# A low table laid out by rows, products joined, squares halved, and a second order by hand

## The chip, the cores and the metric

The kernel runs on one core of one Trainium2 chip. The metric is device time in microseconds (us): the median of several runs of the compiled kernel. Beside the runs there is one profiled execution, whose span (first to last instruction) and engine times the views below come from. The engines are PE (matrix multiply), DVE (elementwise on tensors), ACT (functions and copies), POOL (here only memsets) and SP (here only the issuing of transfers).

## The reference

Two independent layers over a sequence of 2048 rows of 448 columns, side by side in the output. The first is linear attention with learned feature maps; the second a state-space convolution:

```python
    # first: q, k, v from x @ wqkv, 16 heads of 28
    pq, pk = einsum("bhsd,hdf->bhsf", q, w_phi), einsum("bhsd,hdf->bhsf", k, w_phi)
    phi = concat([softmax(p), softmax(-p)])            # of pq and of pk
    kv, z = einsum("bhsf,bhsd->bhfd", phi_k, v), phi_k.sum over s
    a = ((phi_q @ kv) / (phi_q . z + 1e-6)) @ wo
    # second: 448 channels, 256 states each
    dt = exp(log_dt); logdA = dt * (A_re + 1j * A_im)
    P = exp(logdA[:, :, None] * l)                     # l = 0..2047, rounded to bf16
    K = einsum("dn,dnl,dn->dl", Cc, P, dt * Bc).real
    b = irfft(rfft(u) * rfft(K)) + u * Dskip
```

The rounding of l to bf16 leaves 640 distinct positions besides 0, so K is needed at 640 places and not at 2048.

## The kernel before

The kernel splits the position l into a high part (`HI`, 16 values) and a low part (`LO`, 40 values), so that z^l = z^high * z^low for each state's z = exp(logdA). `tables(qt)` does one quarter qt of the channels (QC = 224 columns: 56 pairs of channels by their states) in this order: `rotations` and `dampings` (ACT: sines and exponentials of small multiples), `hi_tables` (DVE: the high table U_ by doubling with z^16, z^32, z^64, z^128), `damp` (DVE: rows 2 to 15 of the low table W as amplitude times rotation), `far` (DVE and ACT: rows 16 to 39), `build_k` (PE: the sum over states, U_ against W, copied out of PSUM) and `scatter_k` (SP: the result to DRAM and back, put by position into KT).

`far` makes rows of W from other rows. A `step(s0, d0, n)` multiplies n complex rows from s0 on by z^256 into rows d0 on: two multiplies (one by the imaginary part into a scratch tile t, one by the real part into W), then a subtraction and an addition. `squares` makes four complex squares: real and imaginary parts squared (two calls of ACT's Square, or DVE), the product of the two parts (DVE) doubled (`scaled`, ACT or DVE), and the difference of the squares (DVE). W is [128, 2, 40, 224]: all rows of the real part, then all of the imaginary part. The powers of z, `PW[k]`, lie as [128, 2, 896].

Around the tables lie the other stages. `signal_spectrum(b)` transforms the signal u against the cosine table G1 on PE and stores it in DRAM. `key_side` makes the attention's sums over keys: per pair of blocks two matmuls, exponentials on ACT, a DMA transpose, matmuls for the softmax sums, a reciprocal and a product on DVE (L612, L613), and matmuls that add up. `query_side(sc)` makes one block of 512 queries: small DVE operations on the scores (L657 to L663), their transpose stored to DRAM by SP and read back four times as SB (L667, L670), and two DVE products by it (L673). `kernel_spectrum(qt)` transforms KT on PE, block b=0 and b=1; its copies go to SK. `conv(qt)` multiplies the two spectra (`prod`, L732, three of 3584 elements), sums real and imaginary parts (`finish`, L738 to L741, or on PE in `finish_pe`), and transforms back (`inverse`).

The order is written out by hand. Every operation is recorded in `Prog` with its engine; at the end `prog.run(ORDER)` issues the recorded operations in the order of a list of numbers, and each engine takes its own in that sequence. `PICKS` holds a letter for each copy, square or scaling that could be on either engine (A is ACT, V is DVE). `PLACES` holds the SBUF address of each tile, and `SLOTS` the PSUM banks. An instruction waits for a count of another engine (or of its own) or for a DMA queue's count; SP's transfers rotate over eight such counts, so that a transfer is issued when the eighth ahead of it has landed. The recording helpers have one line each, so in the views L177 is any two-input DVE operation, L205 any copy, L208 any scaling, L211 any Square, L198 any other activation, L220 any matmul.

Of the kernel before, what the change touches and what calls it, by code (L numbers as in the profile page):

```python
# [10 lines left out]
F32 = mybir.dt.float32  # L11
# [10 lines left out]
N_LO = 40  # L22
# [13 lines left out]
N_KT = 5  # L36
ON_PE = [(0, 1), (1, 1)]
SPLIT = [[(0, QC)]] * 4
# [11 lines left out]
def _dft_tables():  # L50
# [69 lines left out]
def kernel(  # L120
# [227 lines left out]
    q128, q256 = (sb([128, 2, NCOL], F32) for _ in range(2))  # L348
# [16 lines left out]
    for k in LOWP:  # L365
        af(by_states(cs[k][:, 0, :]), from_states(bT), ACT.Sin, scale=float(k), bias=bias_hp)
        af(by_states(cs[k][:, 1, :]), from_states(bT), ACT.Sin, scale=float(-k if k == 8 else k))
        mul(PW[k] if k != 128 else q128, cs[k], amp[k].unsqueeze(1).to_broadcast([128, 2, NCOL]))
        if k == 128:
            copy(PW[128], q128)  # L370
    s2 = sb([128, 2, NCOL], F32)
    square(s2, q128)
    sub(q256[:, 0, :], s2[:, 0, :], s2[:, 1, :])
    stt(q256[:, 1, :], q128[:, 0, :], -2.0, q128[:, 1, :], ALU.mult, ALU.mult)
    copy(view(PW[256][:, 0, 0:1], [56, 32], [1, 2], [2, 28]), view(q256[:, 0, 0:1], [56, 32], [28, 2], [1, 28]))
# [76 lines left out]
    WS = N_LO * QC  # L452
# [41 lines left out]

    def damp(W, A, T, qt, x0, w):
        scaled(A[:, 2:21:3, x0:x0 + w], A[:, 1:20:3, x0:x0 + w], -1.0)
        for part in (1, 0):
            copy(view(W[:, part, 1, x0:x0 + 1], [56, w // 56], [2, 28], [1, 2]),
                 view(PW[8][:, part, qt * QC + x0:qt * QC + x0 + 1], [56, w // 56], [1, 28], [28, 2]))
            mul(view(W[:, part, 2, x0:x0 + 1], [2 * QC, 7], [QC, 2], [1, w]),  # L500
                view(A[:, 0, x0:x0 + 1], [3 * QC, 7], [(1 + part) * QC, 2], [1, w]),
                view(T[:, part, 0, x0:x0 + 1], [QC, 7], [0, 2], [1, w]))

    def far(W, qt, x0, w):
        def pw(i, n):
            return view(PW[256][:, i, qt * QC + x0:qt * QC + x0 + 1], [0, 2], [0, n], [1, w])

        def at(part, row, n):
            return view(W[:, part, row, x0:x0 + 1], [WS, 2], [QC, n], [1, w])

        def rows_(part, row, n):
            return view(W[:, part, row, x0:x0 + 1], [QC, n], [1, w])

        def step(s0, d0, n):
            t = sb([128, 2, n, w])
            mul(t, at(0, s0, n), pw(1, n))
            mul(at(0, d0, n), at(0, s0, n), pw(0, n))
            sub(rows_(0, d0, n), rows_(0, d0, n), t[:, 1])
            add(rows_(1, d0, n), rows_(1, d0, n), t[:, 0])

        def squares(s0, ka, kb, d0):
            def four(part, row, a, b):
                return view(W[:, part, row, x0:x0 + 1], [a * QC, 2], [b * QC, 2], [1, w])
# [6 lines left out]
        copy(view(W[:, 0, 16, x0:x0 + 1], [WS, 2], [1, w]),  # L530
             PW[256][:, :, qt * QC + x0:qt * QC + x0 + w])
# [6 lines left out]
    def hi_tables(qt):  # L538
# [14 lines left out]
        for i, o in ((1, t), (0, U_[:, :, 8:16])):  # L553
            times(o, U_[:, :, 0:8], PW[128][:, i, cols], 16)
# [4 lines left out]
    def build_k(W, U_, TS, c):  # L559
        for j0, nj in ((0, 4), (4, 3)):  # L560
            (b,) = prog.banks(1)
            for j in range(nj):
                items = []
                for i in range(4):
                    nch, ri = i // 2, i % 2
                    for g in range(4):
# [4 lines left out]
                                      view(W[:, ri, 0, x:x + 1], [QC, N_LO], [1, 2]),  # L571
# [215 lines left out]
    def tables(qt):  # L787
# [3 lines left out]
        W = sb([128, 2, N_LO, QC])  # L791
        TS = sb([128, N_LO, 28])
        mset(W[:, 0, 0, :], 1.0)
        mset(W[:, 1, 0, :], 0.0)
        for x0, w in SPLIT[qt]:
            damp(W, A, T, qt, x0, w)
            far(W, qt, x0, w)
            for c in range(x0 // 112, (x0 + w) // 112):
                build_k(W, U_, TS, c)
# [115 lines left out]
```

## Time and profile before

| | |
|---|---|
| median of 3 runs | 238.38 us (238.07 to 239.37) |
| span of the profiled execution | 235.7 us |
| PE busy, matmuls | 208.2 us, 3044 |
| DVE busy, instructions | 218.3 us, 276 |
| ACT busy, instructions | 183.7 us, 312 |
| bytes moved, mean rate | 36.40 MB, 154 GB/s |
| granted TensorE clock | 1.00 all through |

The span and the busy times are of the profiled execution; the runs are 2.7 us longer than its span. Busy time counts a moment once even if two instructions of an engine overlap in it. PE's instructions are pipelined and their ends are modelled, so its busy share does not mean that it is at its limit: in the groups the matmuls of 128x112 take 213 ns, those of 128x448 355 ns.

### The profile page before, as it was taken

How to read it: one execution, taken by the hardware profiler on the slowest of the kernel's cores; microseconds unless marked ns; L12 is line 12 of the kernel's file. 1: busy time of each engine (PE TensorE's matmuls, PEld its weight loads, DVE VectorE, ACT ScalarE, POOL GpSimd, SP SyncE). 2: the span in 40 equal slices, each digit the busy share in tenths (PEclk: the TensorE clock that was granted, in tenths of full speed). 3: DMA queues.
4: the chain of work that ended last, by engine and by line, in shares of the span. 5: the costliest groups of instructions: out<-in, count | busy, mean ns of one | idle time of the engine just before them, and what ended most of it. 6: DMA issues, size and time to landing. Idle time of an engine off the chain costs nothing.

```text
span 235.7 us, 7111 instructions
## 1 busy us (share of the span) xinstructions
PE 208.2 (88%) x3044; PEld 152.1 (65%) x3044; DVE 218.3 (93%) x276; ACT 183.7 (78%) x312; POOL 4.7 (2%) x20
## 2 busy tenths in 40 slices
PE   1338799999898899999998999999999988999993
PEld 2225344656458468677766769765599956787993
DVE  1999999999999899989999999999999899995981
ACT  2999999999999999999999999993337725315420
POOL 2000000000000100000000000000000000000000
PEclk9999999999999999999999999999999999999999
DMA  5899792482978256986449399825784996475952
GB/s 147 213 204 287 132 211 45 157 207 65 298 159 103 59 134 147 178 154 203 139 115 209 25 157 283 217 47 46 234 266 103 165 121 207 32 203 125 209 107 63
DMA packets 81640, 36.40 MB, mean 154 GB/s; under 512 B 65480, under 2 KB 79688, under 8 KB 81224
## 3 DMA queue, kind: packets, MB, share of 16 engines
q1 hardware_dynamic: 81368, 35.71, 69.9%
q8 instruction: 24, 0.39, 0.8%
q10 hardware_dynamic: 240, 0.23, 0.3%
q14 instruction: 8, 0.07, 0.1%
HBM read 19.44 MB, written 8.62 MB: 119 GB/s over the span
## 4 chain that ended last, share of the span: by engine, by line
ACT 28%; DVE 18%; PE 11%; issue 7%; DMA 5%; SPq 0%; DVEq 0%; ACTq 0%
DVE sbuf L177 17%; ACT sbuf L198 13%; PE psum L220 11%; ACT sbuf L205 8%; DMA sbuf<-SCd 4%; ACT sbuf L211 4%; ACT L198 2%; ACT sbuf L208 2%; DMA SCd<-sbuf 1%; SPq L240 0%; DVE sbuf L194 0%; DVE sbuf L189 0%; DVE sbuf L205 0%; DVEq L177 0%; ACTq L198 0%
## 5 line engine op out<-in xcount | busy, mean ns | idle before, releaser
L220 PE MATMUL psum<-sbuf 128*128 128x112 bf16 (+9 forms) x3000 | 206.6, 251 | 23.7 <-ACT sbuf L205 8.8
L177 DVE TENSOR_TENSOR sbuf<-sbuf 128x896 bf16<-128x896 bf16 (+14 forms) x222 | 198.5, 956 | 9.9 <-ACT sbuf L198 5.1
L220 PEld LDWEIGHTS <-sbuf 128*128 128x128 bf16 (+3 forms) x3000 | 149.8, 114 | 79.1 <-issue 16.0
L205 ACT CAST sbuf<-psum 128x448 bf16<-128x448 f32 (+4 forms) x125 | 79.2, 704 | 41.2 <-PE psum L220 40.6
L198 ACT ACTIVATE sbuf<-psum 128x448 bf16<-128x448 f32 (+4 forms) x110 | 63.2, 713 | 1.8 <-PE psum L220 1.7
L211 ACT ACTIVATE sbuf<-sbuf 128x896 bf16<-128x896 bf16 (+1 forms) x16 | 16.5, 1085 | 2.8 <-issue 2.8
L198 ACT ACTIVATE sbuf<-psum,sbuf 128x896 f32<-128x896 f32 (+3 forms) x17 | 13.7, 817 | 0.0
L198 ACT ACT_TABLE_LOAD x8 | 10.3, 1283 | 1.4 <-PEq L899 1.2
L208 ACT ACTIVATE sbuf<-sbuf 128x896 bf16<-128x896 bf16 (+1 forms) x9 | 11.1, 1230 | 0.3 <-DVE sbuf L177 0.3
L205 DVE CAST sbuf<-psum 128x448 bf16<-128x448 f32 (+2 forms) x12 | 7.8, 669 | 2.4 <-PE psum L220 2.4
L215 POOL MEMSET sbuf<- 128x224 bf16 (+4 forms) x15 | 4.3, 314 | 150.4 <-PE psum L220 114.5
L205 ACT COPY sbuf<-psum 112x896 bf16<-112x896 bf16 (+2 forms) x12 | 6.7, 584 | 0.0
L205 ACT COPY sbuf<-sbuf 128x224 bf16<-128x224 bf16 (+2 forms) x13 | 6.1, 476 | 0.0
L177 DVE TENSOR_TENSOR sbuf<-psum,sbuf 128x448 bf16<-128x448 f32 (+3 forms) x12 | 5.0, 442 | 0.0
L194 DVE RECIPROCAL sbuf<-psum 128x64 bf16<-128x64 f32 x8 | 4.4, 549 | 0.2 <-PE psum L220 0.2
L230 PE MATMUL psum<-sbuf 112*112 112x112 bf16 (+1 forms) x44 | 3.5, 216 | 0.0
L230 PEld LDWEIGHTS <-sbuf 112*112 112x112 bf16 (+1 forms) x44 | 2.9, 129 | 0.5
L194 DVE RECIPROCAL sbuf<-sbuf 128x64 f32<-128x64 f32 x4 | 2.2, 545 | 0.0
L189 DVE SCALAR_TENSOR_TENSOR sbuf<-sbuf 128x64 f32<-128x64 f32 (+1 forms) x5 | 1.9, 390 | 0.0
L205 ACT CAST sbuf<-sbuf 128x1792 bf16<-128x1792 f32 x1 | 1.7, 1706 | 0.0
L208 DVE TENSOR_SCALAR sbuf<-sbuf 128x896 bf16<-128x896 bf16 (+2 forms) x4 | 1.6, 401 | 0.0
L205 DVE COPY sbuf<-sbuf 128x448 bf16<-128x448 bf16 (+1 forms) x5 | 1.3, 269 | 0.0
(10 smaller groups left out, 3.0 us busy)
## 6 DMA issues: line engine op xcount, KB each, us to landing
SUd<-sbuf SPq DMA_DIRECT2D x8, 448.0 KB
sbuf<-SCd SPq DMA_DIRECT2D x16, 224.0 KB
sbuf<-SUd SPq DMA_DIRECT2D x4, 896.0 KB
sbuf<-const SPq DMA_DIRECT2D x3, 1024.0 KB
sbuf<-const SPq DMA_DIRECT2D x8, 384.0 KB
sbuf<-in_B_u_dram SPq DMA_DIRECT2D x4, 448.0 KB
out_dram<-sbuf SPq DMA_DIRECT2D x4, 448.0 KB
out_dram<-sbuf SPq DMA_DIRECT2D x16, 112.0 KB
```

Of the source, the lines that this page charges most:

```text
L177: prog.add("V", lambda: nc.vector.tensor_tensor(out=o, in0=a, in1=b, op=op))
L189: prog.add("V", lambda: nc.vector.scalar_tensor_tensor(out=o, in0=a, scalar=s, in1=b, op0=op0, op1=op1))
L194: nc.vector.reciprocal(o, a)
L198: prog.add("A", lambda: nc.scalar.activation(o, a, fn, **kw))
L205: either(lambda: nc.scalar.copy(o, a), lambda: nc.vector.tensor_copy(o, a))
L208: either(lambda: nc.scalar.activation(o, a, ACT.Copy, scale=s), lambda: nc.vector.tensor_scalar_mul(o, a, s))
L211: either(lambda: nc.scalar.activation(o, a, ACT.Square), lambda: nc.vector.tensor_tensor(out=o, in0=a, in1=a, op=ALU.mult))
L215: prog.add("G", lambda: nc.gpsimd.memset(o, v))
L220: nc.tensor.matmul(o, lhsT=l, rhs=r, **kw)
L230: nc.tensor.transpose(o, i, idn)
```

## The change

The change has four parts.

The layout: W becomes [128, 40, 2, 224], the two parts of each row side by side, and the powers PW, q128, q256 and s2 become [128, 4, 2, 224], by quarter. `build_k` reads W with a stride of 448 elements instead of 224.

Joined products: where rows ahead in W can serve as the scratch (n rows behind the destination), a `step` makes both multiplies in one instruction of twice the size: the first step of 7 rows (2 x 3136 become 6272) and the first of 4 rows (2 x 1792 become 3584). The last step of 4 rows has no rows ahead and keeps two. In `hi_tables` the levels 16, 32 and 64 each make one multiply of two. `damp` makes one copy of two; TM is made by two multiplies of 1792 instead of one of 3584.

Halved squares: one activation squares both parts of four rows with a scale of 2^-0.5, which gives half of each square; the doubling of the product goes. Rows so made are smaller by a factor of 2 (and of 8 in the second round), which the constant table F takes back (`GROWN`).

A second order: `ORDER`, `PLACES`, `SLOTS` and `PICKS` are new. The kernel records 969 operations instead of 1008. DVE has 251 instructions instead of 276, ACT 298 instead of 312; PE's 3044 matmuls and the 158 transfers of SP and ACT remain.

```diff
+HALF = 2.0 ** -0.5
+GROWN = {3: 2.0, 4: 8.0}
...
-            F[blk, kt, r] += np.stack([even.real, odd.real, even.imag, odd.imag])
+            F[blk, kt, r] += GROWN.get(kt, 1.0) * np.stack([even.real, odd.real, even.imag, odd.imag])
...
-    PW = {k: sb([128, 2, NCOL]) for k in (8, 16, 32, 64, 128, 256)}
+    PW = {k: sb([128, 4, 2, QC]) for k in (8, 16, 32, 64, 128, 256)}
...
-    mul(TM, CR.unsqueeze(1).to_broadcast([128, 2, 2, NCOL]), PW[8].unsqueeze(2).to_broadcast([128, 2, 2, NCOL]))
+    for i in range(2):
+        mul(TM[:, i].rearrange("p c (q x) -> p c q x", q=4), CR.rearrange("p c (q x) -> p c q x", q=4),
+            PW[8][:, :, i, :].unsqueeze(1).to_broadcast([128, 2, 4, QC]))
...
+    def damp(W, A, T, qt):
+        scaled(A[:, 2:21:3], A[:, 1:20:3], -1.0)
+        copy(view(W[:, 1, 0, 0:1], [56, 8], [2, 28], [1, 2]), view(PW[8][:, qt, 0, 0:1], [56, 8], [1, 28], [28, 2]))
         for part in (1, 0):
...
         def step(s0, d0, n):
-            t = sb([128, 2, n, w])
-            mul(t, at(0, s0, n), pw(1, n))
-            mul(at(0, d0, n), at(0, s0, n), pw(0, n))
-            sub(rows_(0, d0, n), rows_(0, d0, n), t[:, 1])
-            add(rows_(1, d0, n), rows_(1, d0, n), t[:, 0])
+            if d0 + 2 * n <= N_LO:
+                t = W[:, d0 + n:d0 + 2 * n]
+                mul(view(W[:, d0, 0, 0:1], [2 * n * QC, 2], [QC, 2 * n], [1, QC]),
+                    view(W[:, s0, 0, 0:1], [0, 2], [QC, 2 * n], [1, QC]),
+                    view(PW[256][:, qt, 0, 0:1], [QC, 2], [0, 2 * n], [1, QC]))
+            else:
+                t = sb([128, n, 2, QC])
+                for o, i in ((t, 1), (W[:, d0:d0 + n], 0)):
+                    mul(o.rearrange("p n i x -> p (n i) x"), W[:, s0:s0 + n].rearrange("p n i x -> p (n i) x"),
+                        PW[256][:, qt, i, :].unsqueeze(1).to_broadcast([128, 2 * n, QC]))
+            sub(W[:, d0:d0 + n, 0, :], W[:, d0:d0 + n, 0, :], t[:, :, 1, :])
+            add(W[:, d0:d0 + n, 1, :], W[:, d0:d0 + n, 1, :], t[:, :, 0, :])
 
         def squares(s0, ka, kb, d0):
-            sq = [sb([128, 4, w]) for i in range(2)]
-            for i in range(2):
-                square(sq[i].rearrange("p (a b) x -> p a b x", a=2), four(i, s0, ka, kb))
-            mul(four(1, d0, 2, 1), four(0, s0, ka, kb), four(1, s0, ka, kb))
-            scaled(rows_(1, d0, 4), rows_(1, d0, 4), 2.0)
-            sub(rows_(0, d0, 4), sq[0], sq[1])
+            sq = sb([128, 4, 2, QC])
+            af(sq.rearrange("p (a b) i x -> p a b (i x)", a=2), four(s0, 0, 2, ka, kb), ACT.Square, scale=HALF)
+            mul(four(d0, 1, 1, 2, 1), four(s0, 0, 1, ka, kb), four(s0, 1, 1, ka, kb))
+            sub(W[:, d0:d0 + 4, 0, :], sq[:, :, 0, :], sq[:, :, 1, :])
...
             t = sb([128, 2, 8, n, 2, 28])
-            for i in range(2):
-                times(t[:, i], U_[:, :, s0:s0 + n], PW[k][:, i, cols], 2 * n)
+            mul(t.rearrange("p r s n i x -> p r s (n i) x"),
+                view(U_[:, 0, s0, 0, 0:1], [0, 2], [N_HI * 56, 8], [28, 2 * n], [1, 28]),
+                view(PW[k][:, qt, 0, 0:1], [QC, 2], [28, 8], [0, 2 * n], [1, 28]))
...
-                                      view(W[:, ri, 0, x:x + 1], [QC, N_LO], [1, 2]),
+                                      view(W[:, 0, ri, x:x + 1], [2 * QC, N_LO], [1, 2]),
...
-        W = sb([128, 2, N_LO, QC])
+        W = sb([128, N_LO, 2, QC])
...
-    "3 0 41 1 2 42 44 60 35 62 61 5 30 33 58 49 8 9 43 50 59 7 52 55 51 53 57 6 54 80 81 71 63 47 56 48 45 70 82 78 "
+    "35 1 2 67 0 3 5 41 42 44 45 43 49 6 50 60 9 58 52 53 51 7 54 56 62 8 57 61 70 55 65 71 39 77 78 40 46 4 37 63 "
...
```

More of the change, by code (lines that the diff above doesn't have):

```diff
@@ L36 @@
 N_KT = 5
+HALF = 2.0 ** -0.5
+GROWN = {3: 2.0, 4: 8.0}
 ON_PE = [(0, 1), (1, 1)]
-SPLIT = [[(0, QC)]] * 4
 def _round_bf16(a):
@@ L344 @@
     LOWP = (128, 16, 8, 32, 64)
-    PW = {k: sb([128, 2, NCOL]) for k in (8, 16, 32, 64, 128, 256)}
+    PW = {k: sb([128, 4, 2, QC]) for k in (8, 16, 32, 64, 128, 256)}
     amp = {k: sb([128, NCOL], F32) for k in LOWP}
     cs = {k: sb([128, 2, NCOL], F32) for k in LOWP}
-    q128, q256 = (sb([128, 2, NCOL], F32) for _ in range(2))
+    q128, q256 = (sb([128, 4, 2, QC], F32) for _ in range(2))
     CR = sb([128, 2, NCOL])
@@ L451 @@
     ANGLES = [(4, 1, 3, 1), (2, 2, 0, 2), (1, 4, 1, 1)]
-    WS = N_LO * QC
     def args(src, qt):
@@ L493, in dampings @@
         return A
-    def damp(W, A, T, qt, x0, w):
-        scaled(A[:, 2:21:3, x0:x0 + w], A[:, 1:20:3, x0:x0 + w], -1.0)
+    def damp(W, A, T, qt):
+        scaled(A[:, 2:21:3], A[:, 1:20:3], -1.0)
+        copy(view(W[:, 1, 0, 0:1], [56, 8], [2, 28], [1, 2]), view(PW[8][:, qt, 0, 0:1], [56, 8], [1, 28], [28, 2]))
         for part in (1, 0):
[L498 to L502, printed above, removed]
@@ new lines, in damp, with far, four @@
+            mul(view(W[:, 2, part, 0:1], [4 * QC, 7], [2 * QC, 2], [1, QC]),
+                view(A[:, 0, 0:1], [3 * QC, 7], [(1 + part) * QC, 2], [1, QC]),
+                view(T[:, part, 0, 0:1], [QC, 7], [0, 2], [1, QC]))
+    def far(W, qt):
+        def step(s0, d0, n):
+            if d0 + 2 * n <= N_LO:
[10 more added lines that the diff above has]
+            add(W[:, d0:d0 + n, 1, :], W[:, d0:d0 + n, 1, :], t[:, :, 0, :])
+        def squares(s0, ka, kb, d0):
+            def four(row, part, n, a, b):
+                return view(W[:, row, part, 0:1], [2 * a * QC, 2], [2 * b * QC, 2], [1, n * QC])
+            sq = sb([128, 4, 2, QC])
+            af(sq.rearrange("p (a b) i x -> p a b (i x)", a=2), four(s0, 0, 2, ka, kb), ACT.Square, scale=HALF)
+            mul(four(d0, 1, 1, 2, 1), four(s0, 0, 1, ka, kb), four(s0, 1, 1, ka, kb))
+            sub(W[:, d0:d0 + 4, 0, :], sq[:, :, 0, :], sq[:, :, 1, :])
+        copy(W[:, 16], PW[256][:, qt])
@@ L553, in hi_tables @@
         for i, o in ((1, t), (0, U_[:, :, 8:16])):
-            times(o, U_[:, :, 0:8], PW[128][:, i, cols], 16)
+            times(o, U_[:, :, 0:8], PW[128][:, qt, i, :], 16)
         sub(U_[:, :, 8:16, 0, :], U_[:, :, 8:16, 0, :], t[:, :, :, 1, :])
@@ L790, in tables @@
         A = dampings(qt)
-        W = sb([128, 2, N_LO, QC])
+        W = sb([128, N_LO, 2, QC])
         TS = sb([128, N_LO, 28])
         mset(W[:, 0, 0, :], 1.0)
[L794 to L799, printed above, removed]
+        mset(W[:, 0, 1, :], 0.0)
+        damp(W, A, T, qt)
+        far(W, qt)
+        for c in range(2):
+            build_k(W, U_, TS, c)
         scatter_k(qt, TS, KT[qt])
```

26 lines of the change are left out of this document (8 added, 18 removed), and 100 rows, old and new, of tables (ORDER, PLACES, SLOTS).

## The prediction

> **What bounds the kernel now.** I read the page's busy times and slices first, then the table of waits, then the chain of waits at its end, then the groups by line with shapes kept apart.
>
> ```profile
> PE 208.2 (88%) x3044; PEld 152.1 (65%) x3044; DVE 218.3 (93%) x276; ACT 183.7 (78%) x312; POOL 4.7 (2%) x20
> ...
> DVE  1999999999999899989999999999999899995981
> ACT  2999999999999999999999999993337725315420
> ```
>
> DVE is full in every slice between the first and the last few. ACT is as full for two thirds of the span and half empty after. So the question is what DVE does and what it waits for. In the table of waits (engine and line waiting, what released it, total us, times, longest) DVE's rows are:
>
> ```profile
> DVE sbuf L177 <- ACT sbuf L198: 5.1, 3, 4.1
> ...
> DVE sbuf L177 <- ACT sbuf L205: 2.6, 2, 2.4
> DVE sbuf L205 <- PE psum L220: 2.4, 2, 1.3
> ...
> DVE sbuf L177 <- ACT sbuf L211: 0.6, 1, 0.6
> DVE sbuf L177 <- DMA sbuf<-SCd: 0.6, 1, 0.6
> ...
> DVE sbuf L194 <- PE psum L220: 0.2, 1, 0.2
> ```
>
> They sum to 11.5 us. 4.1 (the first dt) and 1.3 (the first matmuls) are start-up; 1.0 of the third row comes after the last finish; 2.4 is one wait at 212 to 215 us. That leaves 2.7 us of small waits in the middle. The chain of waits (start, length, what) shows the 2.4 and what follows it:
>
> ```profile
> 199.47 14.29 PE psum L220 x207
> 213.78 0.98 ACT sbuf L205 x2
> 214.78 2.03 DVE sbuf L177
> 216.91 4.18 DVE sbuf L177 x5
> 221.65 2.56 DVE sbuf L177 x2
> 224.24 2.04 DVE sbuf L177
> 226.30 1.17 DVE sbuf L177 x2
> 227.49 0.64 DVE sbuf L177
> ```
>
> PE runs the last quarter's kernel spectrum behind other work, ACT copies it, and only then DVE's first product (214.78) starts. Now read the joints. 221.65 is an 896 and a 3584 that don't need each other: 0.614 + 2.019 = 2.63 by the rows below, yet the pair takes 2.56, so neighbours overlap by 0.077 (the groups agree: 44 instructions of 1081 ns make 47.6 us, but 46.4 busy). 224.24 is the add that needs the product directly ahead: it starts 0.03 after that one's end, with no overlap. 216.91 starts 0.10 after its product. So a DVE instruction that needs the one right ahead costs 0.11 us (0.077 + 0.034) or, where another wait sits on it too, 0.18 (0.077 + 0.10). This is the row that decides my forecast.
>
> ```profile
> L177 DVE TENSOR_TENSOR sbuf<-sbuf 128x1792 bf16<-128x1792 bf16 x44 | 46.4, 1081 | 0.5 <-ACT sbuf L205 0.3
> L177 DVE TENSOR_TENSOR sbuf<-sbuf 128x3584 bf16<-128x3584 bf16 x23 | 46.1, 2019 | 2.4 <-ACT sbuf L205 2.4
> L177 DVE TENSOR_TENSOR sbuf<-sbuf 128x896 bf16<-128x896 bf16 x74 | 43.5, 614 | 1.1 <-ACT sbuf L211 0.6
> ...
> L211 ACT ACTIVATE sbuf<-sbuf 128x896 bf16<-128x896 bf16 x15 | 14.7, 1038 | 2.8 <-issue 2.8
> ...
> L208 ACT ACTIVATE sbuf<-sbuf 128x896 bf16<-128x896 bf16 x6 | 6.3, 1044 | 0.3 <-DVE sbuf L177 0.3
> ```
>
> From 614 to 1081 ns, 896 more elements cost 467: 0.521 ns an element and 147 ns fixed, or 70 once the overlap is taken off. So two multiplies joined save 0.07 us.
>
> **The change, part by part.** The sum is made on the profiled execution: span 235.7 against a median run of 238.38, so 2.7 us lie around it, and I add differences to 238.38.
>
> *Joined multiplies.* Per quarter `far`'s 3136 pair and its first 1792 pair become one each, as do three pairs of `hi_tables`: 5 instructions fewer, 20 in all, 20 x 0.07 = -1.4 us of DVE. No row has 6272 elements or this form (one input broadcast over two dimensions). Lower bound: by the line above, 3.41 us; upper: the f32 row of 1792 (2.02 us), twice the pace, +3.2 us each. The nearest rows are products of 3584 that already broadcast both inputs and lie on the line (2019 against 2014), so I take the line.
>
> *Squares by the scale.* Six ACT scalings of 896 (1044) and two on DVE (about 0.4 by the L208 DVE row) go; pairs of Squares (1038 each) become one of 1792, which the f32 Square's row, 1794, prices. ACT loses about 6 x 0.87 + 8 x 0.2 = 6.8 us. A Copy with a scale (1044) costs what a Square without does (1038), so the scale is free.
>
> *Engine choices.* Onto DVE: the f32 Square of z^128 (f32 row of that size, 2.02), the cast of PW[128] (1.17 by the other such cast), one damping scale (0.6), two spectrum copies (0.6 each), one build copy. Off it: one bf16 Square (0.61), the two scalings, two AT copies (0.55 each), six small copies (0.2 each). Net of these about +2.0. TM's product in two: +0.07. All DVE work together +0.6 us (-1.4 + 2.0), give or take 0.7.
>
> *The new order on DVE.* The listing of the built kernels says which instructions wait on DVE's own count for the instruction directly ahead. Before it is 14 of 276, and none of them ahead of 174 us: the order put something between every product and its sums. After it is 77 of 251: a product and its subtraction, the subtraction and the square, R and VR, all in a row. Two of the 77 lie in the start-up. 15 carry a further wait. (75 - 15) x 0.115 + 15 x 0.18 = 9.6 against 11 x 0.115 + 3 x 0.18 = 1.8 before: +7.8. Where the further wait is long satisfied the price may be the lower (+6.8), and for query-side instructions of 64 elements the overlap lost may be less than 0.077 (lower end +6.2). I take +7.3.
>
> [...]
>
> *Waits that go.* DVE, slower by 0.1 us each step, falls behind what it waited for. The mid waits' 2.7 us go, and with some 12 waits 12 x 0.077 of lost overlap: -3.6. The 2.4 us at 212: from the last table's end DVE has 19.6 us of work to its first product, now plus six joints, 20.3; PE's queue from the first `build_k` matmul to the last first-block spectrum is 18.2 us by its pitches (19.0 before, and the query multiply it waited for at 200 us is done 30 us earlier), then a copy of 0.6: no wait. -2.4.
>
> *Waits that come.* CR's second copy moves ahead of other work on DVE and stands directly behind PE's last raw product: +0.5, with every start-up product queued behind it. On SP, seven of x's transposes, PID and all of u pass ahead of G1 (1 MB); in the first 24 us the DMA engines moved 215 GB/s, and 5.4 MB up to G1's end make 25 us, or 30 if the transposes go slower. DVE gives the spectrum its first input at about 27 (21 us of work and 6 of waits; before 22), so PE starts its heavy phase some 4 us later. Its cover: PE has 197 us of streaming in 236, DVE gets the key side's sums about 16.6 us of queue after PE, and PE may run 23 to 24 us late in its queue before that costs DVE anything; 27 - 8 = 19, plus the 3 to 5 it lost up to there before. The first query block's four SB reads now stand behind the next block's score store on SP (issue about 122, needed about 130; landing took 6 to 10 us): 0 to 2. Together I take +0.9. POOL's memsets are far ahead of their users. `build_k` reads W at twice the stride; no row shows that, its 896 matmuls (256 ns) may cost nothing or, if a tenth more, 0.4 in the last quarter.
>
> Sum: +0.6 + 7.3 - 3.6 - 2.4 + 0.9 = +2.8, so 241.2 us (span 238.5).
>
> **The rivals.**
> (1) *A wait on the instruction ahead costs nothing in the middle of the kernel*, where the trace has none. Then DVE stays in front of ACT and PE and keeps about 1 us of the old waits: 0.6 - 3.6 - 2.4 + 1 + 0.9 = -3.5, 234.9, faster. For it: ACT's 7 us and the shorter tail queue are real. Against: ten joints of plain kind in the trace and not one without its 0.11. It decides below 0.045 us a joint. 8%. [...]
> (2) *Half is absorbed*: joints 0.06 on average, +3.8 in place of 7.3: 237.7; or the work sums to 0.7 less and the joints take their lower end: 239.4. About no change. 14%.
> (3) *The late start bites*: G1 or u lands after 32 rather than 27. Each us beyond some 30 then shifts PE's key side and DVE one for one: at 33, +3, 244. For it: 1 MB moved behind seven transposes on queues that are 90% busy. Against: it starts as soon as the eighth transfer ahead has landed, while before it waited for a DVE read till 17. 14%.
> (4) *The joined multiply isn't cheaper*: 6272 and the five-dimensional 3584 off the line by a fifth, some 24 us of such work: +5, 246. Nothing in the rows speaks for it. 3%.
>
> **How the numbers follow.** The forecast has 61%. A measurement of this kernel can't tell less than 0.5% (1.2 us: 237.2 to 239.6) from no change. Faster: 8% and a little of (2), 10%. Same: the rest of (2) and the forecast's lower edge, 13%. Slower 77%. Range: below 238.0 lies 12%, above 244.0 some 8%; the forecast's own is 239.6 to 243.0.
>
> **What would show it.** In the profile after: DVE's 251 instructions busy for some 223 us although their work grows by 0.6 only (busy time counts an overlap once, so each joint adds its 0.077); no wait of DVE over 1 us between the start-up and the last finish; runs of DVE in the timeline broken by gaps of 0.03 to 0.1 at products and their sums; the 2.4 us before the last quarter's first product gone; ACT near 175. Wrong would be: DVE's neighbours overlapping although one waits for the other (1), a wait of DVE L194 or L177 on PE of over 1 us at 75 to 100 us (3), a joined 3136 pair over 3.6 us (4).

## The result and the profile after

The changed kernel takes 246.74 us (median of 4 runs, 244.60 to 248.04) against 238.43 us before: a ratio of 1.0345, with a 95% interval of 1.0288 to 1.0403. It is slower, as forecast, but by 8.3 us where 2.8 were forecast, and the time lies above the range. Ratios, here and below, compare fast runs alone, while a median is of all runs, so a ratio is not always the quotient of the two medians beside it. The profiled execution has a span of 245.4 us (235.7 before); it belongs to the run of 247.50 us. In the runs of this study one run takes 1.6 to 2.1 us more than its own span, not the 2.7 that the prediction took from a span and a median of different runs. Its page, busy times and slices:

```profile
PE 214.0 (87%) x3044; PEld 154.8 (63%) x3044; DVE 224.0 (91%) x251; ACT 178.6 (73%) x298; POOL 4.7 (2%) x20
...
PE   1354899999999999999798989998699999999973
...
DVE  1899999999999999999997999999797999999981
ACT  2989999999999998999987769767405545233320
...
PEclk9999999999999999999999999999799999999999
```

DVE is busy for 5.7 us longer with 25 instructions fewer. New are the 7s in its row at slices 22, 29 and 31, and one 7 in the granted clock of TensorE, in slice 29, behind a 6 in PE's own row. The helpers stand one line further down in this kernel: L178 is any two-input DVE operation, L206 any copy, L221 any matmul. The table of waits (engine and line waiting, what released it, total us, times, longest) names the waits behind these slices:

```profile
PE psum L221 <- issue: 4.3, 3, 3.3
...
DVE sbuf L178 <- PE psum L221: 1.7, 1, 1.7
DVE sbuf L178 <- ACT sbuf L206: 1.6, 1, 1.6
DVE sbuf L178 <- DMA sbuf<-SCd: 1.6, 1, 1.6
...
DVE sbuf L178 <- DVE sbuf L206: 0.2, 1, 0.2
```

The wait of the last quarter's product, 2.4 us of the row "DVE sbuf L177 <- ACT sbuf L205: 2.6" of before, is gone; what is left of it is the 0.2 of the last line (the 1.6 behind ACT here is another product's). In its place stand three single waits of 1.6 to 1.7 us: at 134.07 for the score reads of query block 0, at 174.49 (the damping of quarter 3) for PE, at 187.50 (the product of quarter 1) for a copy that follows PE. The last two have one origin, which the chain of waits shows (start, length, what):

```profile
166.28 4.46 PE psum L221 x193
170.74 3.35 issue
174.09 12.33 PE psum L221 x80
186.93 0.55 ACT sbuf L206
187.50 2.57 DVE sbuf L178 x2
```

PE stops for 3.35 us in the middle of one `build_k` operation (8 of its 16 matmuls are done), with no semaphore that it waits for. In the busy times by stretch (us, PE, PEld, DVE, ACT, POOL with instructions, granted clock, DMA share, GB/s), cut at the stop:

```profile
150.00:170.70 20.70, 20.58 (x359) 14.34 (x357) 20.46 (x23) 16.12 (x24) 0.00 (x0) 1.00 0.76 172
170.70:174.10 3.40, 0.05 (x6) 0.01 (x4) 2.13 (x2) 0.62 (x1) 0.00 (x0) 1.00 1.22 188
174.10:177.70 3.60, 3.60 (x26) 2.20 (x27) 3.21 (x2) 2.57 (x6) 0.50 (x2) 0.53 1.05 437
```

In the second row PE is busy for 0.05 us and the DMA engines' share is 1.22; in the third the clock that PE is granted is 0.53 over 3.6 us (by the clock records 0.50 for 3.41 us from 174.28 on). In the kernel before PE never stops for more than 1.2 us after 82 us (the longest is the 1.16 us at 198.31), and its clock is 1.00 all through.

The joints (DVE instructions that need the one directly ahead) are seen in DVE's timeline (start, length; one row is a run of one form without a gap):

```profile
100.55 0.55 DVE L195 RECIPROCAL sbuf<-psum 128x64 bf16<-128x64 f32 x1
101.13 3.06 DVE L178 TENSOR_TENSOR sbuf<-sbuf 128x1792 bf16<-128x1792 bf16 x4
104.11 0.55 DVE L195 RECIPROCAL sbuf<-psum 128x64 bf16<-128x64 f32 x1
104.69 4.41 DVE L178 TENSOR_TENSOR sbuf<-sbuf 128x1792 bf16<-128x1792 bf16 x5
```

The reciprocal of 104.11 starts 0.08 us before the run ahead of it ends (101.13 + 3.06 = 104.19): these neighbours, of which neither needs the other, overlap. Each product that needs its reciprocal (101.13, 104.69) starts 0.03 us after that has ended.

Whole rows of DVE add up to the span, and that is the best way to see where the time went. Busy time is the page's; gaps under 0.15 us before an instruction are short gaps, longer ones waits; the tail runs from DVE's end to the span's end (all us, added up from the traces of this and the experiments):

| | joints | busy | short gaps | waits up to 25 us | waits later | tail | span |
|---|---|---|---|---|---|---|---|
| before | 14 | 218.3 | 1.1 | 6.1 | 5.4 | 4.9 | 235.7 |
| after | 77 | 224.0 | 3.3 | 6.1 | 6.8 | 5.3 | 245.4 |
| e1 | 77 | 223.9 | 3.6 | 6.2 | 7.5 | 4.5 | 245.6 |
| e2 | 33 | 219.8 | 1.6 | 11.1 | 8.7 | 5.0 | 246.2 |
| e3 | 77 | 224.2 | 3.3 | 5.9 | 9.8 | 5.1 | 248.3 |
| e4 | 77 | 224.3 | 3.4 | 5.9 | 6.7 | 4.9 | 245.2 |
| e5 | 16 | 216.5 | 0.8 | 6.2 | 8.0 | 4.6 | 236.1 |
| e6 | 57 | 222.1 | 2.6 | 6.1 | 5.4 | 5.1 | 241.3 |
| e7 | 38 | 220.2 | 1.8 | 6.1 | 3.9 | 4.7 | 236.7 |
| e8 | 77 | 223.9 | 3.3 | 6.0 | 3.5 | 5.1 | 241.8 |
| e9 | 57 | 222.0 | 2.6 | 6.1 | 2.3 | 5.1 | 238.1 |
| e10 | 39 | 220.6 | 2.0 | 6.1 | 8.2 | 5.1 | 242.1 |
| e13 | 14 | 218.8 | 0.9 | 6.2 | 6.7 | 4.5 | 237.1 |
| e14 | 16 | 216.7 | 0.8 | 6.2 | 9.0 | 4.6 | 237.2 |

After against before: busy and short gaps +7.9, waits +1.5, tail +0.4, together (but for rounding) the 9.7 us between the two spans. Each row is one execution. Those of e5 and e9 were the fastest of their runs (237.80 against a median of 238.88, 240.10 against 241.76), that of e10 the slowest (243.90 against 242.51), so spans of different rows differ by more, or less, than the medians do.

### The profile page after: what moved, and what is told of

It reads as the page before. It is cut to its first block, busy times and chain, and to the rows that moved or that the text cites. A ratio compares the mean times of both kernels' runs of the same rounds, so it can differ in the third digit from the quotient of the medians.

```text
span 245.4 us, 7066 instructions
## 1 busy us (share of the span) xinstructions
PE 214.0 (87%) x3044; PEld 154.8 (63%) x3044; DVE 224.0 (91%) x251; ACT 178.6 (73%) x298; POOL 4.7 (2%) x20
## 4 chain that ended last, share of the span: by engine, by line
DVE 43%; PE 21%; ACT 16%; DMA 10%; issue 7%; SPq 1%; DVEq 0%; ACTq 0%
DVE sbuf L178 41%; PE psum L221 20%; ACT sbuf L199 9%; ACT sbuf L206 6%; DMA sbuf<-const 4%; DMA sbuf<-SCd 3%; DMA sbuf<-sbuf 2%; DMA sbuf<-in_B_A_re_dram 2%; DVE sbuf L195 1%; SPq L241 1%; ACT L199 1%; DVE sbuf L206 0%; DVE sbuf L209 0%; DVEq L178 0%; DVE sbuf L190 0%
## 5 line engine op out<-in xcount | busy, mean ns | idle before, releaser
L221 PE MATMUL psum<-sbuf 128*128 128x112 bf16 (+8 forms) x3000 | 212.0, 254 | 24.8 <-DVE sbuf L178 11.3
L178 DVE TENSOR_TENSOR sbuf<-sbuf 128x896 bf16<-128x896 bf16 (+12 forms) x203 | 200.7, 1037 | 11.7 <-ACT sbuf L199 3.4
L221 PEld LDWEIGHTS <-sbuf 128*128 128x128 bf16 (+3 forms) x3000 | 152.5, 115 | 82.1 <-issue 18.4
L206 ACT CAST sbuf<-psum 128x448 bf16<-128x448 f32 (+4 forms) x125 | 77.4, 679 | 53.1 <-PE psum L221 51.8
L199 ACT ACTIVATE sbuf<-sbuf 128x1792 bf16<-128x1792 bf16 (+1 forms) x9 | 13.8, 1537 | 2.2 <-DMA sbuf<-in_B_log_dt_dram 1.5
L206 DVE CAST sbuf<-psum 128x448 bf16<-128x448 f32 (+2 forms) x12 | 7.9, 674 | 3.4 <-PE psum L221 3.4
L206 ACT COPY sbuf<-sbuf 128x448 bf16<-128x448 bf16 (+1 forms) x14 | 7.8, 572 | 3.2 <-PE psum L221 3.2
L206 ACT COPY sbuf<-psum 112x896 bf16<-112x896 bf16 (+2 forms) x13 | 6.9, 533 | 2.6 <-DVE sbuf L178 2.1
L178 DVE TENSOR_TENSOR sbuf<-psum,sbuf 128x448 bf16<-128x448 f32 (+3 forms) x12 | 4.9, 439 | 0.0
L209 ACT ACTIVATE sbuf<-sbuf 128x1568 bf16<-128x1568 bf16 x2 | 3.1, 1544 | 0.0
L206 DVE CAST sbuf<-sbuf 128x1792 bf16<-128x1792 f32 x2 | 2.3, 1126 | 0.0
L213 DVE TENSOR_TENSOR sbuf<-sbuf 128x1792 f32<-128x1792 f32 x1 | 2.0, 2017 | 0.0
L209 DVE TENSOR_SCALAR sbuf<-sbuf 128x1568 bf16<-128x1568 bf16 (+1 forms) x3 | 1.5, 504 | 0.0
## 6 DMA issues: line engine op xcount, KB each, us to landing
sbuf<-SCd SPq DMA_DIRECT2D x16, 224.0 KB
```

Source lines behind the costliest of these rows:

```text
L178: prog.add("V", lambda: nc.vector.tensor_tensor(out=o, in0=a, in1=b, op=op))
L199: prog.add("A", lambda: nc.scalar.activation(o, a, fn, **kw))
L206: either(lambda: nc.scalar.copy(o, a), lambda: nc.vector.tensor_copy(o, a))
L209: either(lambda: nc.scalar.activation(o, a, ACT.Copy, scale=s), lambda: nc.vector.tensor_scalar_mul(o, a, s))
L213: lambda: nc.vector.tensor_tensor(out=o, in0=a, in1=a, op=ALU.mult))
L221: nc.tensor.matmul(o, lhsT=l, rhs=r, **kw)
```

## The experiments

Every kernel was run against the kernel before on the same chip, and each ratio below is to that. The order edits are shown as pieces of an engine's sequence in ORDER, by operation number; unless said otherwise nothing but ORDER differs. In the recorded expectations VectorE is DVE, TensorE is PE and ScalarE is ACT; both names are used from here on.

**e1: the joints alone, in the kernel before.** VectorE's sequence of before, permuted by up to 4 places until it has the changed kernel's 77 joints. One piece of it:

```diff
-630 631 799 633 632 507 508 635 509 634 567 637 566 510
+630 631 633 632 799 507 508 509 566 635 634 637 510 511
```

> The kernel before with nothing but DVE's own sequence changed: neighbours swapped by up to four places, so that 77 of its 276 instructions wait for the one directly ahead (14 before), no load or PE or ACT sequence touched. 63 more joints x 0.117 = 7.4 us. Theory A (a joint costs 0.117 us, and DVE, now later, no longer meets its old waits of 2.7 in the middle and 2.4 at 212 us): 238.4 + 7.4 - 5 = 240.5 to 242. Theory B (the joints cost that, but DVE carries PE and ACT along with it, so the old waits stay): 244.5 to 246. Theory C (a joint is free): 238 to 239.

Measured: 246.84 us, ratio 1.0338 (1.0290 to 1.0386). The time is above what all three theories allowed. The old mathematics with 77 joints is as slow as the changed kernel, but not by its joints alone. By the table busy and short gaps grow by 8.1 us for 63 joints, 0.13 each. The old waits shrink (the last product's from 2.37 to 1.00), but the permutation made one of its own: the queries' small operations came later, and VectorE waited 4.37 us for the score reads of block 0, until 136.72. (PE also waited 3.55 us for a load at 127.23 and had half its clock for 6.83 us from 129.32 on.) The price of a joint is shown; the total isn't a clean sum.

**e2: the joints taken out of the changed kernel.** The same by up to 5 places the other way, 77 down to 33:

```diff
-489 488 490 491 433 435 615 492 493 436 614 772 710 709
+489 488 433 490 491 615 492 435 493 436 614 772 709 710
```

> The changed kernel with DVE's sequence alone altered by swaps of up to five places: 33 joints instead of 77, every other engine's sequence and all transfers as they were. 44 x 0.117 = 5.1 us. Theory A (joints are the largest part of the loss): 246.7 - 5.1 = 241.6, DVE busy down by 44 x 0.077 = 3.4 to some 220.6. Rival (DVE only waits elsewhere, since PE's late second half and the score reads set the time): 244.5 to 246.5 with DVE's idle up by what its joints gave back.

Measured: 247.51 us, ratio 1.0364 (1.0308 to 1.0419). Busy and short gaps fall by 5.8 us for 44 joints, again 0.13 each, and all of it is lost: 5.0 us to waits at the start, where the permutation put instructions ahead of loads and results that they need, and the rest to PE, which stops for 3.27 us at 171.57 and has half its clock for 6.83 us behind it. The time is above both theories. As a test of the total it failed by its own start.

**e3: the score reads of block 0 ahead of the next block's store on SP.**

```diff
-717 497 500 499 465
+497 500 499 717 465
```

> The changed kernel with three of the first query block's four SB reads moved on SP ahead of the next block's score store, behind which they stood. Theory: DVE's wait of 1.6 us on these reads at 132 us goes or shrinks to under 0.4, time -1 to -1.6 (245.1 to 245.7). Rival (it is taken back by the PE stall at 171 us or by the ACT copies behind it): no change, 246.5.

Measured: 248.62 us, ratio 1.0395 (1.0313 to 1.0476). The wait of 1.57 us at 134 goes and comes back as one of 1.65 us at 142, for the reads of the next block. PE's stop stays (3.48 us at 172.09), and the waits of VectorE behind it are longer here (3.02 and 2.73 us). The interval overlaps the changed kernel's, so no change in time is shown: here one block's reads were had sooner at the next block's cost.

**e4: the loads around PE's stop spread.** The stop comes just behind ten transfers that SP issues between 162.4 and 170.2 us: four score reads, three transposed loads of u, a signal spectrum of 896 KB (733) and the two halves of GI (529, 528) of 1 MB each. Four of them moved:

```diff
-882 883 880 881 737 574 733 734 529 528 669 668 940 896 670
+733 574 882 883 880 881 737 734 669 668 940 896 528 529 670
```

> The changed kernel with the burst of loads at 162 to 170 us thinned out on SP: SU of the second quarter and one u transpose go ahead of the third block's SB reads, the two GI loads (1 MB each) go behind the third quarter's scatter. Theory P (PE's stall of 3.35 us in the middle of one build_k operation, at 170.7, is instruction fetch held up by that burst): the stall shrinks to under 1.5, DVE's waits of 1.7 each at 172.8 and 185.9 shrink, time -2 to -3.5 (243 to 245). Rival (the stall comes with the pace of build_k, wherever the loads are): stall still over 2.5, time unchanged or up to 1 us longer, should GI come late for the first inverse.

Measured: 246.74 us, ratio 1.0346 (1.0292 to 1.0400): no change in time. But PE's stop shrank from 3.35 to 0.94 us, no half clock followed it, and the wait of 1.66 us went. GI now came late: PE stood 2.65 us at 182.78 before the first inverse transform, the clock fell to half for 3.41 us behind that, and VectorE waited 1.68, 1.07 and 0.90 us later on. So the stop did what theory P said and the time (243 to 245 us expected) did not: the gain was given back by the cure.

**e5: the mathematics without the order.** The changed kernel's functions with the order, places, banks and engine choices of before, mapped operation by operation. The one edit besides these lists gives the squares' scratch a place in rows of W that are not written yet:

```diff
-            sq = sb([128, 4, 2, QC])
+            sq = W[:, d0 + 4:d0 + 8]
```

> All of the change's mathematics and layouts (rows side by side, joined products, squares halved by the activation's scale, the far copy and the damp copy joined), but in the order of before: each operation stands where before had it, two that were joined where the first of them stood, a halved square where the later of the two squares stood; places, banks and engine choices are those of before, and the squares' scratch lies in rows of the table that are not written yet. 254 VectorE instructions against 276 before and 251 after, and 16 that wait for the one directly ahead (14 before, 77 after). Theory order (the 8.3 us come from the new order alone, its joints and the waits that it makes): the joined products save 1.4 us of VectorE, the scalings and squares that leave it about another 1, so 235.5 to 237.0 us. Theory maths (a product, copy or square costs more in the new form than its row says): 240 us or more. Theory cover (VectorE's saved work only lengthens its waits for TensorE): 238.0 to 238.8 us.

Measured: 238.88 us against 237.93 before, ratio 1.0085 (1.0043 to 1.0127). So all but 1 to 2 of the 8.3 us (0.95 by the medians, 2.0 by the ratio) come with the new order and the places, banks and engine choices that belong to it; these four are not told apart here. The mathematics does save VectorE its 1.8 us (busy 216.5 against 218.3), but the waits grow by 2.7 us. Its rows in the table of waits:

```profile
DVE sbuf L178 <- ACT sbuf L199: 6.6, 7, 4.2
DVE sbuf L178 <- ACT sbuf L206: 3.4, 2, 3.1
```

The first has 4.2 of start-up and 2.4 of exponentials and joined squares that ACT hands over no earlier than before; the second is the last quarter's product, 3.1 where before had 2.4. Of the three theories cover came nearest (238.0 to 238.8 us).

**e6: fewer joints, cleanly.** As e2, but with the first 45 VectorE instructions and those of the queries held in place; 77 down to 57:

```diff
-367 368 770 427 429 428 370 371 373 374 431 612 613 432
+367 368 427 770 429 428 370 371 373 374 612 431 432 613
```

> The changed kernel with VectorE's own sequence permuted by at most 5 places so that 57 instead of 77 instructions wait for the one directly ahead; the first 45 VectorE instructions and those of the queries keep their order, other engines' sequences and the queues are untouched. Theory J (joints are paid on the path that sets the end): 20 x 0.115 = 2.3 us less, 244.4 us. Theory P (TensorE's stop at 171 us and its half clock set the end): VectorE waits instead, 246.0 to 247.4 us.

Measured: 243.69 us against 237.93, ratio 1.0272 (1.0231 to 1.0313). Busy and short gaps fall by 2.5 us, 0.125 a joint, and nothing takes it back. The time falls somewhat further than theory J's 244.4, because the block-0 score wait (1.57 us) is gone as well. PE's stop (3.50 us at 167.43, half clock for 3.41 us) is still there. So these 20 joints were paid on the path that sets the end.

**e7: more joints in the kernel before, cleanly.** 14 up to 38:

```diff
-627 451 626 452 628 453 379 629 380 383 382 455 798 454
+627 626 628 629 451 452 453 379 380 383 382 455 798 454
```

> The kernel before with VectorE's own sequence permuted by at most 6 places so that 35 to 38 instead of 14 instructions wait for the one directly ahead; the first 45 and those of the queries keep their order. Theory J: 22 to 24 x 0.115 = 2.6 us more, less what its middle waits (2.7 us) take up: 239.5 to 241.2 us. Theory hidden (the middle waits take all of it): 238.0 to 239.0 us. Above 242: the permutation made a wait of its own, as in the first such run.

The run had 38. Measured: 238.92 us against 237.93, ratio 1.0048 (1.0024 to 1.0072). 24 joints add 2.6 us of busy and short gaps (0.11 each) and take 1.5 us out of the waits; the span grows by 1.0. The time itself lies in the range of the theory "hidden", but the kernel before was faster in this round than the 238.4 us that the ranges start from; the 1.0 us over it lie between the two theories (up to 0.6, and from 1.1 on). So the waits of this row paid about half of these 24 joints.

**e8: the loads spread without making GI late.**

```diff
-882 883 880 881 737 574 733 734 529 528 669 668 940 896 670 672
+733 574 882 883 880 881 737 734 528 669 668 940 896 670 672 529
```

> The changed kernel with four loads moved on SP: the first quarter's spectrum load and one transposed load stand ahead of the last query block's score reads (some 8 us earlier), the first half of the inverse tables stays, and their second half goes four transfers later. Theory P (TensorE's stop of 3.35 us in the middle of one operation at 171 us is an instruction fetch behind a burst of loads, and the half clock behind it follows from the stop): the stop is under 1.2 us, no half clock follows, the wait of 1.62 us at 187.5 is gone: 243.0 to 245.0 us. If the second half of the tables now comes late, TensorE waits at the first inverse transform instead and the time stays within 246 to 247.5 us. Theory J alone: no change, 246.7 us.

By the edit three loads change place (733, 574 and 529), and the second half of the tables goes six transfers later. Measured: 243.16 us against 237.93, ratio 1.0247 (1.0209 to 1.0284), as theory P had it. PE's timeline at the place of the stop:

```profile
164.83 5.97 PE L221 MATMUL psum<-sbuf 112*128 112x448 bf16 x231
171.65 4.65 PE L221 MATMUL psum<-sbuf 128*32 128x80 bf16 x39 [0.85 <-issue]
```

The stop is 0.85 us, no half clock follows, and both waits of VectorE (1.66 and 1.62) are gone: its waits after 25 us fall from 6.85 to 3.45 us. The stop was worth 2.3 us by the two ratios, 3.1 by the medians (8.3 and 5.2 us over before).

**e9: both edits.** The sequence of e6 with the transfers of e8.

> The changed kernel with both edits that helped: 57 instead of 77 instructions of VectorE that wait for the one directly ahead (the sixth run's sequence), and the loads spread on SP (the eighth run's). Theory two causes (the joints and TensorE's stop with its half clock are separate terms of the 8.3 us): the gains of the two runs, some 3.0 and 3.5 us, add up: 239.7 to 241.0 us against 246.7 of the changed kernel. Theory one cause (either edit only shifts the same wait): no better than the better of the two, 243.0 us or more.

Measured: 241.76 us against 237.63, ratio 1.0158 (1.0126 to 1.0190). By the ratios e6 gains 0.73 points, e8 0.98, both together 1.87, each give or take 0.7. The interval of e9 lies below those of e6 and of e8, so either edit gains on top of the other: joints and stop are two separate causes. That the gains add up in full is not shown so closely: by the medians, each less its own before, they are 2.6, 3.1 and 4.2 us, and 241.76 lies between the two ranges that were expected. VectorE has hardly a wait left in this kernel; its two largest rows:

```profile
DVE sbuf L206 <- PE psum L221: 3.4, 4, 1.3
DVE sbuf L178 <- ACT sbuf L199: 3.4, 1, 3.4
```

Both are start-up and tail but for 0.6 at 202 us. The span of its profiled execution is 2.4 us over before (the medians differ by 4.1): busy and short gaps are 5.2 over, waits 3.1 under.

**e10: 39 joints with the transfers of e8.** A piece against e8:

```diff
-714 774 775 776 617 777 616 618 619 501 502 871 872 873
+714 774 616 775 617 776 777 619 501 618 502 871 872 873
```

> As the ninth run, but with 39 instead of 57 instructions that wait for the one directly ahead; the first 30 VectorE instructions and those of the queries keep their order but for shifts of up to 2 places. Theory J: another 18 x 0.115 = 2.1 us less than the ninth run, 237.6 to 239.2 us. Theory cover (TensorE's own row of work sets the end once VectorE has less to do, as in the fifth run): no less than 239.5 us.

Measured: 242.51 us against 237.63, ratio 1.0211 (1.0184 to 1.0238), no gain. Busy and short gaps fall by another 2.0 us, but VectorE now comes early to score reads (1.21 us at 130, 2.56 at 138) and to a copy behind PE (1.61 at 206). (Its profiled execution also had half the clock from 17.7 to 31.3 us, behind the start-up's stops.) The time is in the range of the theory cover, but its account fits only in part: what came back is waits for transfers and for PE, not PE's row alone.

**e11 and e12: the last quarter's spectrum ahead of an inverse transform on PE.** In the kernel before and in e5, one PE operation moved:

```diff
-772 775 927 947 975 967 963 971 757
+772 775 927 975 967 963 971 947 757
```

> The kernel before with one TensorE operation moved: the inverse transform of 36 matmuls (1.94 us) that stands ahead of the last quarter's first four spectrum operations goes behind them. The last quarter's product, which waits 2.37 us for the copy of their result, then waits some 0.4 us. Theory V (VectorE's row sets the end there): 1.0 to 1.9 us less, 236.0 to 237.0 us. Theory E (TensorE is without gaps there, so its own row sets the end): within 0.5 us of the kernel before.

> The fifth run's kernel (the change's mathematics in the order of before) with the same move on TensorE. Its last quarter's product waited 3.07 us; after the move some 1.1. Theory V: 1.5 to 1.9 us less than the fifth run, and so under the eleventh run by what of the 1.8 us of saved VectorE work is not taken by waits for ScalarE. Theory E: as the fifth run, 238.4 to 239.2 us.

Measured: 238.75 and 239.08 us against 237.63, ratios 1.0044 (1.0023 to 1.0064) and 1.0030 (1.0001 to 1.0058). The first lies above both its theories, the second in theory E's range. The product's wait did not shrink (2.98 and 3.19 us): on ACT, the copy of the moved transform still stood ahead of two of the spectrum's copies and held them up. Here the move on PE's queue alone brought the product nothing (before waits 2.37 us, e5 3.07).

**e13 and e14: the same, with the two copies moved on ACT.**

```diff
-926 754 976 968 948 972 964 928
+926 754 976 968 972 964 948 928
```

> The eleventh run's kernel with two more moves, on ScalarE: the last two of the first four copies of the last quarter's spectrum stand ahead of the copy of the inverse transform that was moved on TensorE, which held them up. The last quarter's product then waits some 0.5 us (2.37 in the kernel before, 2.98 in the eleventh run). Theory V (VectorE's row sets the end): 236.0 to 237.2 us. Theory E (TensorE's row without gaps sets the end, so the wait comes back behind it): 237.3 to 238.8 us, as before.

> The same moves in the kernel with the change's mathematics in the order of before. The product's wait falls from 3.1 to some 1.2 us. Theory V: 236.2 to 237.4 us, and with the 1.8 us of saved work at or under the thirteenth run. Theory E: 237.8 to 239.2 us, as the fifth run.

Measured: 238.33 and 238.72 us against 237.84, ratios 1.0019 (0.9989 to 1.0049) and 1.0023 (0.9995 to 1.0051). The product's wait fell to 0.98 and 1.38 us, and the time did not follow; both lie in theory E's ranges. VectorE's timeline at the end of e13 and then of e14, and PE's in the same order:

```profile
215.14 2.02 DVE L177 TENSOR_TENSOR sbuf<-sbuf 128x3584 bf16<-128x3584 bf16 x1 [0.98 <-ACT sbuf L205]
...
223.64 6.47 DVE L177 TENSOR_TENSOR sbuf<-sbuf 128x3584 bf16<-128x3584 bf16 x6 [0.80 <-ACT sbuf L205]
...
231.99 0.62 DVE L205 CAST sbuf<-psum 128x448 bf16<-128x448 f32 x1 [1.21 <-PE psum L220]
```

```profile
215.14 2.03 DVE L178 TENSOR_TENSOR sbuf<-sbuf 128x3584 bf16<-128x3584 bf16 x1 [1.38 <-ACT sbuf L206]
...
223.64 6.47 DVE L178 TENSOR_TENSOR sbuf<-sbuf 128x3584 bf16<-128x3584 bf16 x6 [0.80 <-ACT sbuf L206]
...
231.99 0.62 DVE L206 CAST sbuf<-psum 128x448 bf16<-128x448 f32 x1 [1.21 <-PE psum L221]
```

```profile
201.60 32.06 PE L220 MATMUL psum<-sbuf 112*128 112x448 bf16 x523 [0.94 <-issue]
...
201.60 32.06 PE L221 MATMUL psum<-sbuf 112*128 112x448 bf16 x523 [1.15 <-issue]
```

The first kernel's VectorE is busy for 2.1 us more than the second's, and both run the end at the same hundredths: PE starts 523 matmuls at 201.60 and runs them without a gap, and there its row, by way of ACT's copies, sets the time. Theory E's "without gaps" holds only from that point on: up to it PE stood 0.94 and 1.15 us with no semaphore to wait for (more on such stops at the end). So the saved VectorE work of the mathematics ends in waits, and the wait taken away before the product comes back as 0.31, 0.80 and 0.17 more behind it (e13). No kernel of this study was faster than the kernel before.

## Why the prediction was right and wrong

*VectorE's work, +0.6: right.* The row that decided the fourth rival stands on the line (3.41 forecast):

```profile
L178 DVE TENSOR_TENSOR sbuf<-sbuf 128x6272 bf16<-128x6272 bf16 x4 | 13.7, 3429 | 0.1
```

Busy time was forecast at some 223 and is 224.0. The durations, less 0.08 us of overlap an instruction, grow by some 1.1 us, within the 0.7 that was allowed either way. The joined Square with its scale costs less than the row that it was priced by (1704 against 1794 ns):

```profile
L199 ACT ACTIVATE sbuf<-sbuf 128x1792 bf16<-128x1792 bf16 x8 | 13.6, 1704 | 0.7 <-DVE sbuf L178 0.6
```

ACT came to 178.6 us, not near 175.

*Joints, +7.3: right.* In the changed kernel's trace 61 plain joints have a median of 116 ns and the 16 with a further wait one of some 185; gaps and lost overlap of all 77 come to some 9.8 us, of the 14 of before to 1.8, so about +8, a little over the 7.8 that was worked out and of which 7.3 were taken. Work and joints together were forecast at +7.9, and busy time and short gaps grew by 7.9. The runs that add or remove joints find 0.11 to 0.13 each. The first rival falls with it: the wait on the instruction ahead is not free in this kernel. The second rival (half absorbed) is what e7 shows for the first 24 joints in the kernel before; in the changed kernel nothing was left to absorb them (e6).

*Waits that go, -3.6 and -2.4: right in kind, too large.* None of the middle waits of before is in the trace after, and the 2.37 us before the last product are 0.20. But the 0.9 us of lost overlap that was to go with the 12 waits did not go: a start without overlap stands behind each wait that came, too.

*Waits that come, +0.9: this step failed.* They are 6.2 us, and the sign "no wait of DVE over 1 us" in the middle fails three times: CR's copy 0.51 (forecast 0.5); the score reads of block 0 1.57 (bounded by 0 and 2, and taken at 0.4 at most); `build_k`'s copy 0.62 and a wait of 0.22 at 138; and 1.66 and 1.62 from PE's stop and its half clock, for which there was no term at all. The stop is the larger half. The prediction followed the transfers that change place only to the data that they carry, and asked when VectorE needs it. The ten transfers at 162 to 170 us do no harm by that test, and yet PE stops behind them, and no longer does (0.85 us in place of 3.35) when three of them are moved (e8). The other assumption under this step was that PE goes through its queue at full speed, so that a VectorE which is 8 us slower could only fall behind it. Without the stop the forecast is still missed: e8 is 5.2 us over before, not 2.8. By the table its waits are 2.0 us under before (9.5 against 11.5), where the three terms on waits had 5.1 under: the wait at 134 us (1.48) and that of `build_k`'s copy (0.58) remain, and the 0.9 of lost overlap was counted in vain.

*The late start of PE (third rival): it doesn't bite.* From 12.45 to 134 us VectorE has no wait of 0.15 us or more, though PE stands four times for 1.0 to 3.1 us between 13.9 and 26.6.

*What was not asked: which part of the change costs.* The forecast priced the mathematics at -1.4 and the scheduling at the rest; e5 agrees that the order, with its engine choices, is what costs, but the mathematics' gain of 1.8 us of VectorE's work did not become time with that order of PE.

*What stays open.* With the loads spread and 57 joints the kernel is 1.6% over before. By the table its busy time and short gaps are 7.3 us over those of e5: the 41 joints more, at 0.12 each, make 4.9, and the other 2.4 fit the work that the new engine choices put on VectorE (forecast at 2.0). Its waits are 5.8 under. An order of the changed kernel without these joints and without new waits was not found (e10 made some), and the engine choices were not tried by themselves, so this split is worked out and not shown.

## What to carry to other kernels

Count, for each engine that is always busy, the instructions that need the one directly ahead; here each cost 0.12 us, and 63 more of them (some 8 us) outweighed all that the new mathematics saved VectorE (1.8 us). When transfers are moved, look at what else the DMA engines carry in that stretch, the instruction transfers too: here PE went on 2.3 to 2.6 us after one of them had started, and had stood for 3.35 us with the loads together and for 0.85 with them spread. And before work is taken off one engine, see whether another one, which also has hardly a gap there, sets the end, as PE's row does from 201.60 on in e13 and e14.

## What the runs showed of the hardware

*PE's stops and the instruction transfers.* The DMA records have instruction transfers of 16 KB (queue q8) all along, 24 in the trace of before and as many in that of after; which engine they are for is not in the records. Where the loads stand together, the transfer that belongs to the stop starts after PE has stopped; where they are spread, before:

| | transfer starts | PE stops at | for | PE goes on at | half clock behind it |
|---|---|---|---|---|---|
| after | 171.5 | 170.7 | 3.35 | 174.1 | 3.41 |
| e2 | 172.4 | 171.6 | 3.27 | 174.8 | 6.83 |
| e3 | 173.2 | 172.1 | 3.48 | 175.6 | 6.83 |
| e6 | 168.5 | 167.4 | 3.50 | 170.9 | 3.41 |
| e10 | 169.4 | 169.9 | 1.87 | 171.7 | none |
| e4 | 169.7 | 171.1 | 0.94 | 172.1 | none |
| e8 | 169.2 | 170.8 | 0.85 | 171.7 | none |
| e9 | 166.2 | 167.8 | 0.92 | 168.7 | none |

In all eight PE goes on 2.3 to 2.6 us after the transfer has started, however long it stood, which ties the stop to the transfer in these runs. Between the two pairs that differ in these loads alone (after and e8, e6 and e9) the transfer starts 2.3 us earlier where the loads are spread, and the stop is 0.85 us in place of 3.35, and 0.92 in place of 3.50; so in these four runs it goes with their place. The trace has no record of when a transfer of this kind is asked for: that it queues behind the loads, and that PE waits for its instructions, is the author's reading of these times and is not shown. Short stops without a semaphore are in the kernel before too, and PE goes on at the same distance: it stops at 198.31 for 1.16 us, with a transfer at 197.14 and the next matmul, which waits for no semaphore, at 199.47. So the prediction's reading of PE's wait at 200 us as one for the query multiply is wrong:

```profile
199.47 28.52 PE L220 MATMUL psum<-sbuf 112*128 112x448 bf16 x451 [1.16 <-issue]
```

The stops ahead of 201.60 in e13 and e14 are of this kind as well (transfers at 199.16 and 199.02).

*The half clock.* Stops of some 3.3 to 3.5 us in the table were followed by 3.41 or 6.83 us at a granted clock of 0.50. What length of stop brings it on is not shown: in e4 stops of 1.44 and of 2.65 us were each followed by 3.41 us of half clock, while 2.85 in e10, 2.68 in e12 and 2.01 in e14 were not, nor were waits of 4.03 and 4.43 us in the start-up of before (at 6.41 for DVE and at 13.61 for ACT), and e5 and e13 each have 3.41 us of half clock at 112.5 and 112.4 us with no stop over 0.6 us near it.

*Overlap of neighbours.* VectorE instructions that don't need each other overlap by some 0.08 us on nearly every row here, products, reciprocals and copies alike (0.2 behind the products of 128x128 and one cast in each of the two traces); this, more than the gap of 0.03, is what a joint loses.
